# Sliding-window attention and a squared-ReLU MLP on one core: the third batch turned on TensorE, no band matmuls, and an instruction order read from a table

## The chip, the core and the metric

The kernel runs on one core of a Trainium2 chip. The metric is the device time of one launch in microseconds (us). The kernel before takes 298.31 us, the median of three runs (298.27 to 298.75).

## What is computed

Eight batches of eight heads, 576 positions, head size 64. Each position attends to the positions at most 32 away. The heads are then laid side by side (512 columns, 4608 tokens), and an MLP without bias follows, with the square of a ReLU between two matrices.

```python
scores = scale * np.matmul(q, k.transpose(0, 1, 3, 2))      # scale = 1/8
mask = np.abs(pos[:, None] - pos[None, :]) <= 32
attn = softmax(np.where(mask, scores, -1e9))
x = np.matmul(attn, v).transpose(0, 2, 1, 3).reshape(4608, 512)
h = x @ w_in                      # 512 x 2048
r = np.maximum(h, 0.0)
out = (r * r) @ w_out             # 2048 x 512, float32 out
```

## The kernel before

**Groups.** The attention is cut into 24 groups G of 192 tokens, three to a batch. Group G loads its rows of q and k (`load_qk`, L537, issued by GpSimd with a cast to bf16) into one of four `raw` buffers, and a window of 256 rows of v (`load_v`, L563) into one of five `v` buffers. The rows have to be turned so that the head dimension lies on the partitions. For batches 0 and 1, TensorE does this by transposing matmuls (`turn_pe`, L596, eight per turned piece) and ScalarE or VectorE copies the result into the buffer `kq` (L607, L608). From batch 2 on, SyncE issues DMAs that transpose while they move (`turn_dma`, L622, two per group). There are two `kq` buffers, for even and odd batches. A `raw` buffer is free for a later load when its rows have been turned.

**Scores and values.** `scores` makes two blocks of keys per group, A and B (L661, eight matmuls a block). For groups 0 to 2 it first adds the band as a matmul of a bias table with the identity (L653, two 128x512 matmuls a block), and ScalarE's exponential is then the end (L677). For all other groups the exponential (L682) is followed by a multiplication with a 0/1 mask on VectorE (L686). `pv` multiplies with v (L712) and VectorE normalises (L726, L730). A clearing copy (L736) readies the PSUM region between the two blocks.

**Turning the result.** The rows of x go into `xt` turned: by TensorE for groups 0 to 5 (`xturn`, L752 and L758, one copy L766 or L768), by transposing DMAs on SyncE from group 6 on (L771, L774).

**MLP.** `xt` feeds the first layer: plain matmuls (`mm1`, L808) for tokens up to 3584, in pieces of 192, 256 and 512 tokens, and a scheme with seven products instead of eight for the last two blocks of 512 (`mm1s`, L870). ReLU (L787) and square (L782) follow. The second layer is plain for the first 512 tokens (`mm2`, L927), and a seven-product scheme for the others (`strassen`, `product`, L1003, with a copy L1035 that seeds the second bank, and copies and sums L792, L1026). ScalarE issues the stores (L939). While data is still coming in, `fill` puts small matmuls on zeros (L462) into TensorE's gaps.

**What sets the order.** Every operation is recorded with its engine, reads, writes and a key. `plan` (L126 on) then runs a list scheduler with assumed durations, picks for each engine the operation that can start first (ties by key), gives out buffers and PSUM banks, and so fixes one instruction sequence per engine. `emit` writes it with semaphore waits. SyncE, GpSimd and ScalarE work through their queues in that order: an instruction that waits holds all behind it. `OPEN` is the order of the first loads.

Of the kernel before, what the change touches and what calls it, by code (L numbers as in the profile page):

```python
# [1 line left out]

# [3 lines left out]
ALU = mybir.AluOpType  # L6
# [18 lines left out]
    BIAS=110.0,  # L25
    LS=12.75,
    LAG=9.0,
    OG=[0.0, 0.25, 2.5, -0.5, 5.25, 3.5, -7.25, -7.5, -9.0, -18.75, -5.5, 9.75, -6.5, -8.25, 1.5, 0.25, -7.25, -8.75, -7.75, -4.5, 4.75, -1.0, -1.75, -0.75],
    OL=[4.25, 5.25, -0.25, 4.0, 2.75, 0.5, 10.75, 9.5, 7.0, -2.25, -2.25, 3.25, -2.0, 5.25, 7.0, -0.25, 5.75, 3.0, 8.75, -0.25, 7.25, -1.5, 3.5, 0.75],
    OS=[6.5, 2.75, -2.25, -4.5, -2.25, 1.25, 0.75, -0.5, -2.25],  # L30
    O1=[6.5, 7.0, 9.75, -1.25, -4.75, 1.0, 6.25, -0.25, -2.0],
    LEAD=13.0,
    AHEAD=14.5,
    NTURN=2,
    NXT=6,
    NSPLIT=6,
    NPM=3,
# [5 lines left out]
    NUE=3,  # L43
    NRT=4,
    NOE=3,
    WARM=40000,
    TSLACK=1000,
    LSLACK=500,
# [18 lines left out]
class Prog:  # L67
# [58 lines left out]
    def plan(self):  # L126
        cfg, ops = self.cfg, self.ops
        for op in ops:
            op.succ, op.left, op.ready = [], 0, 0
        for op in ops:  # L130
            for d in op.deps | op.order:
                d.succ.append(op)
                op.left += 1
            for u in op.uses:
                u.left = len(u.users)
        t = 0
        for op in sorted((o for o in ops if o.eng == "PE"), key=lambda o: (o.key, o.i)):
            op.late = t
            t += op.dur
        for op in reversed(ops):  # L140
            if op.eng == "PE":
                continue
            op.late = min((s.late - (op.lat if op in s.deps else 0) for s in op.succ), default=t + 5000) - op.dur
            if op.eng in ("ACT", "DVE") and op.dma is None and op.key > -50:
                op.key = op.late / 1000 - cfg["BIAS"]
        engs = ("PE", "ACT", "DVE", "POOL", "SP")
        free = {e: 900 for e in engs}
        free["POOL"] = 1350
        cand = {e: [] for e in engs}
        best = {e: None for e in engs}  # L150
        dirty = {e: True for e in engs}
        slots = {}
        for n, k in self.pools.items():
            slots[n] = [[0, None, False] for _ in range(k)]
        bank = slots["bank"]
        warm = cfg["WARM"]
        bank[7][0] = warm
        self.out = out = []
        rings = {"POOL": [], "SP": [], "ACT": []}
        order = ["POOL", "SP", "ACT"]  # L160
        now = spent = 0.0

        def push(op):
            cand[op.eng].append(op)
            dirty[op.eng] = True
            if op.alt:
                cand[op.alt[0]].append(op)
                dirty[op.alt[0]] = True

        def done(op, end):  # L170
            op.end = end
            for s in op.succ:
                if op.dma is not None or op.eng != s.eng or op.eng != "PE":
                    s.ready = max(s.ready, end)
                else:
                    s.ready = max(s.ready, free[op.eng])
                s.left -= 1
                if not s.left:
                    push(s)
            for u in op.uses:  # L180
                u.left -= 1
                u.free = max(u.free, end)
                if not u.left:
                    for x in u.slot:
                        sl = slots[u.pool][x]
                        sl[0] = u.free
                        sl[1] = u
                        if u.pool == "bank":
                            sl[2] = u.clean
                    for e in engs:  # L190
                        dirty[e] = True

        def find(u, taken):
            ss = slots[u.pool]
            if u.pool != "bank":
                got = None
                for x in range(len(ss)):
                    f = ss[x][0]
                    if f < 1e14 and (got is None or f < got[0]) and (u.pool, x) not in taken:
                        got = (f, (x,))  # L200
                return got
            w = u.where if u.where is not None else range(8)
            got = None
            if u.n == 2:
                for x in range(0, 8, 2):
                    if x in w and ("bank", x) not in taken and ("bank", x + 1) not in taken:
                        f = max(ss[x][0], ss[x + 1][0])
                        r = f + (250 if u.need and not ss[x + 1][2] else 0)
                        if f < 1e14 and (got is None or r < got[2]):
                            got = (f, (x, x + 1), r)  # L210
            else:
                for x in w:
                    f = ss[x][0]
                    if f < 1e14 and ("bank", x) not in taken:
                        r = (f, 0 if ss[x ^ 1][0] > 1e14 else 1, x)
                        if got is None or r < got[2]:
                            got = (f, (x,), r)
            return got and got[:2]

        def grab(op, r):  # L220
            taken, res = (), []
            for u in op.acq:
                g = find(u, taken)
                if g is None:
                    return None
                if g[0] > r:
                    r = g[0]
                res.append(g[1])
                taken = taken + tuple((u.pool, x) for x in g[1])
            return r, res  # L230

        def look(e):
            t, pick = None, None
# [947 lines left out]
```

## Time and profile before

| | before |
|---|---|
| median of three runs | 298.31 us |
| the profiled execution | 298.29 us |
| its span (first to last instruction) | 296.5 us |
| mean granted TensorE clock | 0.994 |
| TensorE matmuls busy | 281.7 us (95%) |
| VectorE, ScalarE, GpSimd busy | 213.5, 186.5, 117.4 us |
| moved by DMA | 40.35 MB |

PE is TensorE's matmuls, PEld its weight loads, DVE VectorE, ACT ScalarE, POOL GpSimd, SP SyncE; a letter q behind an engine is its queue of DMA issues. A row of the timeline has the start and duration in us, the engine, the line, what is written from what, how many instructions, and in brackets the idle time ahead of it and what ended that. Matmuls overlap, so that the step from one start to the next is what one costs, not its duration. Some matmul records are missing from the trace: a count of 3 or 7 where the code has 4 or 8.

### The profile page before, as it was taken

How to read it: one execution, taken by the hardware profiler on the slowest of the kernel's cores; microseconds unless marked ns; L12 is line 12 of the kernel's file. 1: busy time of each engine (PE TensorE's matmuls, PEld its weight loads, DVE VectorE, ACT ScalarE, POOL GpSimd, SP SyncE). 2: the span in 40 equal slices, each digit the busy share in tenths (PEclk: the TensorE clock that was granted, in tenths of full speed). 3: DMA queues.
4: the chain of work that ended last, by engine and by line, in shares of the span. 5: the costliest groups of instructions: out<-in, count | busy, mean ns of one | idle time of the engine just before them, and what ended most of it. 6: DMA issues, size and time to landing. Idle time of an engine off the chain costs nothing.

```text
span 296.5 us, 7164 instructions
## 1 busy us (share of the span) xinstructions
PE 281.7 (95%) x2827; PEld 211.6 (71%) x2850; DVE 213.5 (72%) x444; ACT 186.5 (63%) x298; POOL 117.4 (40%) x153
## 2 busy tenths in 40 slices
PE   6989999999599999999999999999999999999995
PEld 5778667877376467646666656666579888888884
DVE  6457869858765786679677877686889799569811
ACT  3577457978536765786577666656875586288330
POOL 8999489856553454456636453200000000000000
PEclk9999999999889999999999999999999999999999
DMA  9999999999999999999999999999612301211133
GB/s 149 170 199 206 187 154 196 154 169 155 137 177 151 176 139 182 188 153 133 165 156 177 166 175 172 152 157 158 136 35 65 123 3 38 71 38 35 38 107 106
DMA packets 178401, 40.35 MB, mean 136 GB/s; under 512 B 165568, under 2 KB 177856, under 8 KB 178368
## 3 DMA queue, kind: packets, MB, share of 16 engines
q0 software_dynamic: 121920, 18.98, 90.4%
q1 hardware_dynamic: 45600, 11.08, 30.2%
q10 hardware_dynamic: 10848, 9.83, 10.8%
q8 instruction: 22, 0.36, 0.5%
q14 instruction: 11, 0.09, 0.1%
HBM read 38.80 MB, written 9.44 MB: 163 GB/s over the span
## 4 chain that ended last, share of the span: by engine, by line
PE 72%; DMA 12%; POOL 9%; ACT 2%; DVE 2%; issue 2%; ACTq 0%; SPq 0%; POOLq 0%; DVEq 0%
PE ps L1003 33%; PE ps L808 24%; PE ps L870 8%; DMA raw<-in_k_dram 6%; DMA kq<-raw 6%; POOL raw L537 4%; PE ps L661 3%; PE ps L712 3%; POOL v L563 3%; POOL w L575 1%; POOL w L570 1%; DVE gt L782 1%; ACT rt L787 1%; ACT ps L1035 0%; ACT oe L792 0%
## 5 line engine op out<-in xcount | busy, mean ns | idle before, releaser
L808 PE MATMUL ps<-xt,w 128*128 128x512 bf16 (+2 forms) x625 | 104.4, 314 | 1.3 <-DMA w<-in_moe_w_in_dram 0.2
L787 ACT ACTIVATE rt<-ps 128x512 bf16<-128x512 f32 (+1 forms) x127 | 71.9, 572 | 37.3 <-PE ps L808 30.2
L808 PEld LDWEIGHTS ps<-xt,w 128*128 128x128 bf16 x640 | 56.5, 98 | 30.5 <-DMA w<-in_moe_w_in_dram 0.4
L782 DVE TENSOR_TENSOR gt<-rt 128x512 bf16<-128x512 bf16 (+1 forms) x112 | 43.6, 404 | 22.5 <-ACT rt L787 20.0
L563 POOL DMA_DIRECT2D v<-in_v_dram x48 | 41.0, 864 | 38.3 <-PE ps L712 34.7
L1003 PE MATMUL ps<-w,gt 128*128 128x256 bf16 x384 | 49.5, 279 | 1.0 <-ACT ps L1035 0.8
L537 POOL DMA_DIRECT2D raw<-in_k_dram x46 | 36.0, 793 | 29.6 <-DMA kq<-raw 27.0
L682 ACT ACTIVATE e<-ps 128x1024 bf16<-128x1024 f32 x42 | 40.9, 1021 | 10.2 <-PE ps L661 10.2
L1003 PEld LDWEIGHTS ps<-w,gt 128*128 128x128 bf16 x384 | 37.4, 100 | 8.7 <-ACT ps L1035 1.1
L537 POOL DMA_DIRECT2D raw<-in_q_dram x46 | 36.0, 790 | 0.8 <-issue 0.8
L686 DVE TENSOR_TENSOR pt<-e,mask 128x1024 bf16<-128x1024 bf16 x42 | 28.4, 686 | 8.6 <-ACT e L682 8.2
L1003 PE MATMUL ps<-ts,gt 128*128 128x256 bf16 x256 | 31.9, 273 | 0.0
L1003 PE MATMUL ps<-ts,ss 128*128 128x256 bf16 x256 | 31.4, 273 | 0.0
L1003 PEld LDWEIGHTS ps<-ts,gt 128*128 128x128 bf16 x256 | 24.9, 98 | 4.7
L1003 PEld LDWEIGHTS ps<-ts,ss 128*128 128x128 bf16 x256 | 24.4, 98 | 4.0
L792 ACT ACTIVATE ue<-ps 128x512 f32<-128x512 f32 x30 | 17.9, 596 | 9.9 <-PE ps L1003 7.4
L792 ACT ACTIVATE oe<-ps 128x512 f32<-128x512 f32 x19 | 11.3, 597 | 17.1 <-PE ps L1003 16.4
L712 PEld LDWEIGHTS ps<-v,pt 128*128 128x128 bf16 x384 | 17.9, 98 | 5.2 <-issue 0.3
L726 DVE RECIPROCAL rs<-ps 64x8 f32<-64x8 f32 (+1 forms) x48 | 10.0, 209 | 15.0 <-PE ps L712 13.9
L712 PE MATMUL ps<-v,pt 128*128 128x65 bf16 x384 | 20.2, 194 | 0.0
L661 PE MATMUL ps<-kq 64*128 64x128 bf16 x384 | 15.9, 217 | 4.2 <-DMA kq<-raw 4.2
L661 PEld LDWEIGHTS ps<-kq 64*128 64x128 bf16 x384 | 10.9, 94 | 12.1 <-issue 8.6
(71 smaller groups left out, 315.0 us busy)
## 6 DMA issues: line engine op xcount, KB each, us to landing
out_dram<-oe ACTq DMA_DIRECT2D x36, 256.0 KB, 6.1
v<-in_v_dram POOLq DMA_DIRECT2D x32, 128.0 KB, 20.8
raw<-in_q_dram POOLq DMA_DIRECT2D x22, 96.0 KB, 19.2
w<-in_moe_w_in_dram POOLq DMA_DIRECT2D x4, 512.0 KB, 10.6
w<-in_moe_w_out_dram POOLq DMA_DIRECT2D x4, 512.0 KB, 17.0
raw<-in_k_dram POOLq DMA_DIRECT2D x14, 112.0 KB, 19.5
v<-in_v_dram POOLq DMA_DIRECT2D x16, 96.0 KB, 19.5
raw<-in_k_dram POOLq DMA_DIRECT2D x16, 96.0 KB, 20.0
```

The source lines that it names most:

```text
L537: self.p.rec("POOL", lambda e, j=j, dst=dst: e.dma_start(dst, s[:, j]), writes=[self.rtag(t, b, g, j)], dma=(f"{t}{G % self.cfg['NRAW']}{j ...
L563: self.p.rec("POOL", lambda e, j=j, lo=lo, hi=hi, k0=k0: e.dma_start(vt[lo - k0:hi - k0, j, :, 0:64], self.v[b, :, lo:hi, :].rearrange("h ...
L661: mm = e.matmul(sc[:, 512 * par + 128 * j:512 * par + 128 * j + 128], kq[r:r + 64, j, k0:k0 + 128], q, start=not pm and j == 0, stop=True, ...
L682: self.p.rec("ACT", lambda e, ef=ef, v=v: e.activation(ef()[:], self.bank(v, 0, 2), ACTF.Exp, scale=0.125), reads=[v], writes=[ev], key=ke ...
L686: self.p.rec("DVE", lambda e, pf=pf, ef=ef, mb=mb: e.tensor_tensor(pf()[:], ef()[:].rearrange("p (h q) -> p h q", h=8), mb, ALU.mult), rea ...
L712: mm = e.matmul(ps[z:z + n, c:c + 65], ptt[:, 4 * (h % 2) + h // 2, z:z + n], vt[:, w, h, 0:65], start=((w == 0 or (z == 64 and split)) an ...
L782: self.p.rec("DVE", lambda e: e.tensor_tensor(dst, src(), src(), ALU.mult), reads=rd, writes=wr, key=key, dur=dve(c), name=name, alt=alt, ...
L787: self.p.rec("ACT", lambda e: e.activation(dst(), src(), ACTF.Relu), reads=rd, writes=wr, key=key, dur=act(c), name=name, alt=alt, bias=se ...
L792: self.p.rec("ACT", lambda e: e.activation(dst(), src(), ACTF.Copy), reads=rd, writes=wr, key=key, dur=act(c), name=name, alt=alt, bias=se ...
L808: mm = e.matmul(ht[:, n * x:n * x + n], self.W1[:, ft, 128 * d:128 * d + 128], self.XT[:, ft, r:r + n], start=(ft == 0 and x == 0), stop=( ...
L870: mm = e.matmul(bk[:, 256 * x:256 * x + 256], lhs(k, 256 * m + 128 * x), rhs[:, k, :], start=start and x == 0 and k == 0, stop=(k == 1), s ...
L1003: mm = e.matmul(op[:, 256 * y:256 * y + 256], lhs[:, l0[0] + k, a:a + 128], rhs[:, r0 + k, c0:c0 + 256], start=start and y == 0 and k == 0 ...
```

## The change

Six things change.

- `turn_pe` turns groups 6 to 8 (batch 2) as well, and `xturn` turns their rows of x on TensorE (`NTG=9`, `NXT=9`). The transposing DMAs of that batch, six of `kq` and six of `xt`, are gone.
- No group has band matmuls (`NPM=0`): groups 0 to 2 take the exponential and mask path of the others.
- q of batch 1 is loaded in the pieces that k has (224, 192 and 160 rows instead of 192 each).
- The first loads stand in another order.
- Buffers: the three `ue` and three `oe` buffers are one pool of six, the four `rt` and two `hb` buffers another.
- `plan` is gone. `apply` reads the engine, the place in time and the buffer of each recorded operation from a string `ORDER`. The numbers there only sort; the waits come from the data and the buffers as before. The durations that `rec` still carries (82 for a weight load, 28.6 for a transposing DMA) no longer set anything.

```diff
-    NTURN=2,
-    NXT=6,
+    NTG=9,
+    PAIR=(),
+    NXT=9,
-    NPM=3,
+    NPM=0,
-    NUE=3,
-    NRT=4,
-    NOE=3,
+    NRT=6,
+    NOE=6,
...
+    def apply(self, order):
+        order = iter(order.split())
+        last = {}
+        for op in self.ops:
+            s = next(order)
+            op.start = int(s[1:])
+            e = "PADGS".index(s[0])
+            op.eng_ = ("PE", "ACT", "DVE", "POOL", "SP")[e]
+            if op.eng_ != op.eng:
+                op.dur, op.fn = op.alt[1], op.alt[2]
+            op.eng = op.eng_
+        virts = dict.fromkeys(u for op in self.ops for u in op.uses)
+        for u in virts:
+            s = next(order)
+            u.wash = s[-1] == "w"
+            u.slot = tuple(range(int(s.rstrip("w")), int(s.rstrip("w")) + u.n))
+        self.out = sorted(self.ops, key=lambda o: (o.start, o.i))
+        for op in self.out:
             for u in op.acq:
...
                 for x in u.slot:
+                    old = last.get((u.pool, x))
+                    if old is not None:
+                        op.order.update(old.users)
+                    last[u.pool, x] = u
...
     def piece(self, t, b, g):
-        return (192 * g, 192) if t == "q" and b < self.cfg["NTURN"] else KC[g]
+        return (192 * g, 192) if t == "q" and not b else KC[g]
...
-            pe = b < cfg["NTURN"]
+            pe = G < cfg["NTG"]
             turn = 0.6 if pe else 3
...
-        self.p.plan()
+        self.p.apply(ORDER)
...
+OPEN = [("k", 0, "SP", "DVE", 0), ("q", 0), ("k", 1), ("q", 1), ("k", 2), ("q", 2, "ACT", "ACT", 2), ("v", 0), ("v", 1),
+        ("w1", 0), ("w1", 1), ("w1", 2), ("w1", 3), ("w2", 1), ("w2", 0), ("v", 2), ("w2", 2), ("w2", 3)]
+ORDER = """
+D900 G2138 A1350 D2835 D3355 D3775 D4195 D4825 D5245 D5665 D6085 D1100 D2130 D1845 D2350 D1460 D2550 D3055 D5045 D5445
...
```

(Only a line of the table is shown.) How this moves instructions is seen at three places.

**TensorE at the scores of group 8.** In the listings a name's number is its buffer; `kq0` holds the even batches. The kernel before, from a piece of the plain second layer to the first pair of products of the seven-product scheme; the second `ps<-kq0` row is group 8's scores:

```order
L927 MATMUL ps<-w2,gt 128x512 x4
L661 MATMUL ps<-kq0 128x128 x16
L808 MATMUL ps<-xt,w1 128x256 x8
L927 MATMUL ps<-w2,gt 128x512 x8
L712 MATMUL ps<-v2,pt2 128x65 x8
L661 MATMUL ps<-kq0 128x128 x16
L712 MATMUL ps<-v2,pt0 128x65 x8
L1003 MATMUL ps<-w2,gt 128x256 x16
```

And the changed kernel, where L417 is `turn_pe`, L482 the scores, L533 `pv`, L573 and L579 `xturn` and L632 `mm1`:

```order
L573 MATMUL ps<-ident,xa0 128x64 x4
L417 MATMUL ps<-ident,raw0 128x80 x8
L579 MATMUL ps<-ident,xb1 128x128 x4
L533 MATMUL ps<-v1,pt2 128x65 x8
L417 MATMUL ps<-ident,raw0 128x80 x8
L632 MATMUL ps<-xt,w1 128x256 x16
L579 MATMUL ps<-ident,xb0 128x128 x4
L482 MATMUL ps<-kq0 128x128 x16
L632 MATMUL ps<-xt,w1 128x256 x8
L632 MATMUL ps<-xt,w1 128x512 x8
```

The two turns of group 8 (`raw0`) and the turns of x now stand on TensorE, sixteen first-layer matmuls lie between the second turn and the scores, and first-layer matmuls of 512 columns follow where the seven-product scheme began.

**TensorE at the scores of batch 5.** `kq1` now holds batch 5; the kernel before, from group 15's scores (the first `ps<-kq1` row) to group 16's (the last):

```order
L661 MATMUL ps<-kq1 128x128 x16
L1003 MATMUL ps<-w2,gt 128x256 x8
L808 MATMUL ps<-xt,w1 128x512 x8
L712 MATMUL ps<-v0,pt0 128x65 x8
L1003 MATMUL ps<-ts1,ss1 128x256 x8
L808 MATMUL ps<-xt,w1 128x512 x4
L1003 MATMUL ps<-ts1,ss1 128x256 x8
L808 MATMUL ps<-xt,w1 128x512 x4
L712 MATMUL ps<-v0,pt1 128x65 x8
L1003 MATMUL ps<-ts0,ss0 128x256 x8
L808 MATMUL ps<-xt,w1 128x512 x4
L661 MATMUL ps<-kq1 128x128 x16
```

In the changed kernel (L826 is the seven-product scheme) from group 14's scores, the row with `kq0`, on; here the first `kq1` row is group 16's scores and the second is group 15's:

```order
L482 MATMUL ps<-kq0 128x128 x16
L826 MATMUL ps<-ts2,gt 128x256 x8
L826 MATMUL ps<-w2,gt 128x256 x8
L826 MATMUL ps<-ts2,gt 128x256 x8
L482 MATMUL ps<-kq1 128x128 x16
L826 MATMUL ps<-w2,gt 128x256 x8
L826 MATMUL ps<-ts3,gt 128x256 x16
L826 MATMUL ps<-w2,gt 128x256 x16
L533 MATMUL ps<-v4,pt1 128x65 x8
L482 MATMUL ps<-kq1 128x128 x16
```

Group 16's scores, which read the turned rows of groups 15 and 16, have moved ahead of group 15's, to three half products behind group 14's.

**SyncE's queue from its first transposing DMA on.** The kernel before; `kq0` is batch 2 at first, and `kq1` batch 3:

```order
L622 DMA_TRANSPOSE kq0<-raw2 128x8x112 x2
L622 DMA_TRANSPOSE kq0<-raw3 128x8x96 x2
L622 DMA_TRANSPOSE kq0<-raw0 128x8x80
L771 DMA_TRANSPOSE xt<-xa0 128x4x64
L622 DMA_TRANSPOSE kq0<-raw0 128x8x80
L774 DMA_TRANSPOSE xt<-xb0 128x4x128
L622 DMA_TRANSPOSE kq1<-raw1 128x8x112 x2
L771 DMA_TRANSPOSE xt<-xa1 128x4x64
L774 DMA_TRANSPOSE xt<-xb1 128x4x128
L771 DMA_TRANSPOSE xt<-xa2 128x4x64
L774 DMA_TRANSPOSE xt<-xb2 128x4x128
```

The changed kernel (L443 is `turn_dma`, L592 and L595 are `xturn`), where the first row is already batch 3 and `kq0` batch 4:

```order
L443 DMA_TRANSPOSE kq1<-raw1 128x8x112 x2
L443 DMA_TRANSPOSE kq1<-raw2 128x8x96
L443 DMA_TRANSPOSE kq1<-raw3 128x8x80
L443 DMA_TRANSPOSE kq1<-raw2 128x8x96
L443 DMA_TRANSPOSE kq1<-raw3 128x8x80
L592 DMA_TRANSPOSE xt<-xa0 128x4x64
L443 DMA_TRANSPOSE kq0<-raw0 128x8x112 x2
L443 DMA_TRANSPOSE kq0<-raw1 128x8x96
L595 DMA_TRANSPOSE xt<-xb0 128x4x128
```

Batch 3's six transposes stand together with none of `xt` between them, and batch 4's come behind the first half of group 9's x (`xa0`).

More of the change, by code (lines that the diff above doesn't have):

```diff
@@ L570, in load_w1 @@
         self.p.rec("POOL", lambda e: e.dma_start(self.W1[:, :, 512 * d:512 * d + 512], src),
-                   writes=[("w1", d)], dma=(f"w1{d}", 0), key=key, dur=780, move=(32, 79), name=f"w1{d}")
+                   writes=[("w1", d)], dma=(f"w1{d}", 0), key=key, dur=780, move=(32, 82), name=f"w1{d}")
     def load_w2(self, d, key):
@@ L575, in load_w2 @@
         self.p.rec("POOL", lambda e: e.dma_start(self.W2[:, 4 * d:4 * d + 4, :], src),
-                   writes=[("w2", d)], dma=(f"w2{d}", 0), key=key, dur=780, move=(32, 79), name=f"w2{d}")
+                   writes=[("w2", d)], dma=(f"w2{d}", 0), key=key, dur=780, move=(32, 82), name=f"w2{d}")
     def turned(self, t, b, g, x=None):
@@ L801, in mm1, with f @@
         gsteps = [(t0 // 64 + x) % (GRING // 64) for x in range(n // 64)]
[L802 to L816 removed]
+        nb = 2 if pair else 1
+        v = Virt("bank", nb, clean=c >= 512, where=self.cfg.get("MB"))
+        for h in range(nb):
+            dh = ds[h:h + 1] if pair else ds
+            def f(e, h=h, dh=dh):
+                ht = self.bank(v, h)
+                for x, d in enumerate(dh):
+                    for ft in range(4):
+                        mm = e.matmul(ht[:, n * x:n * x + n], self.W1[:, ft, 128 * d:128 * d + 128], self.XT[:, ft, r:r + n],
+                                      start=(ft == 0 and x == 0), stop=(ft == 3), skip_group_check=True)
+                return mm
+            self.p.rec("PE", f, reads=[("xt", s) for s in steps] + [("w1", d // 4) for d in dh[:1]], writes=[(v, h)], uses=[v], key=key + 0.25 * h,
+                       dur=4 * len(dh) * (n / 2.4 + 2.5), name=f"A{t0}.{dh[0]}")
+        rt = Virt("rt", nb)
+        tags = [(v, h) for h in range(nb)]
+        self.relu(lambda: self.rt(rt)[:, 0:c], lambda: self.bank(v, 0, nb)[:, 0:c], tags, [rt], key, f"r{t0}.{d0}", c, uses=[v])
+        self.square(lambda: self.rt(rt)[:, 0:c].rearrange("p (d t) -> p d t", d=len(ds)),
                     gt[:, d0:d0 + len(ds), rg:rg + n], [rt], [("gt", s, d) for s in gsteps for d in ds], key, f"g{t0}.{d0}", c)
@@ L932, in mm2 @@
         oe = Virt("oe")
-        self.copy(lambda: self.OE[oe.slot[0]][:], lambda: self.bank(v), [v], [oe], key, f"o{u}")
-        self.store(u, oe, self.out[128 * u:128 * u + 128, :], lambda: self.OE[oe.slot[0]][:], key, (8, 80))
+        self.copy(lambda: self.oe(oe), lambda: self.bank(v), [v], [oe], key, f"o{u}")
+        self.store(u, oe, self.out[128 * u:128 * u + 128, :], lambda: self.oe(oe), key, (8, 42))
     def store(self, u, oe, dst, src, key, move):
@@ L1118, in record @@
             m = 512 // n
+            if t0 in cfg["PAIR"]:
+                for x in range(8):
+                    d = 2 * (x // 2) + 8 * (x % 2)
+                    key = t0 / 64 + x + cfg["O1"][t0 // 512]
+                    at(t0 / 64 + x, self.mm1, t0, n, [d, d + 1], key, True)
+                t0 += n
+                continue
             for x, d in enumerate(range(0, 16, m)):
```

393 lines of the change are left out of this document (138 added, 255 removed), and 8 rows, old and new, of the table ORDER.

## The prediction

> **What bounds the kernel now.** I read the page first, then TensorE's waits, its timeline around the longest of them, and the windows there.
>
> ```profile
> PE 281.7 (95%) x2827; PEld 211.6 (71%) x2850; DVE 213.5 (72%) x444; ACT 186.5 (63%) x298; POOL 117.4 (40%) x153
> DMA  9999999999999999999999999999612301211133
> ```
>
> TensorE is busy for 95% of the span, so it is the engine that sets the end, and the DMA engines are full until about slice 29, some 210 us. Time can go only where TensorE stands still, runs slowly or has work taken from it. TensorE's waits name two sources of size:
>
> ```profile
> PE ps L661 <- DMA kq<-raw: 4.2, 2, 3.6
> PE ps L1003 <- ACT ps L1035: 0.8, 2, 0.4
> ```
>
> The scores (L661) wait twice for transposing DMAs. TensorE's timeline has the places:
>
> ```profile
> 63.90 0.62 PE L661 MATMUL ps<-kq 64*128 64x128 bf16 x16 [0.59 <-DMA kq<-raw]
> ...
> 75.21 0.42 PE L712 MATMUL ps<-v,pt 128*128 128x65 bf16 x8
> 79.20 0.62 PE L661 MATMUL ps<-kq 64*128 64x128 bf16 x16 [3.58 <-DMA kq<-raw]
> ...
> 80.06 3.53 PE L1003 MATMUL ps<-w,gt 128*128 128x256 bf16 x16
> ...
> 84.26 1.92 PE L1003 MATMUL ps<-w,gt 128*128 128x256 bf16 x16 [0.42 <-ACT ps L1035]
> ```
>
> Both are scores of the third batch, groups 6 and 8, and the rows of that batch are what the change turns on TensorE. Sixteen products take 3.53 us right behind the long wait and 1.92 us a little later: the wait has a tail. The windows say why:
>
> ```profile
> 19.00:75.00 56.00, 54.27 (x654) 42.55 (x658) 43.07 (x95) 40.00 (x67) 43.19 (x56) 1.00 1.88 176
> 75.00:80.00 5.00, 1.42 (x33) 1.11 (x32) 3.37 (x7) 1.47 (x4) 1.86 (x4) 1.00 1.82 126
> 80.00:83.50 3.50, 3.50 (x25) 2.55 (x22) 2.66 (x5) 1.80 (x2) 2.25 (x3) 0.52 1.50 203
> 75.00:210.00 135.00, 129.49 (x1163) 85.86 (x1177) 98.70 (x197) 87.36 (x136) 56.20 (x72) 0.99 1.76 163
> ```
>
> The columns are the window, its length, busy PE, PEld, DVE, ACT and POOL, the granted clock, the DMA share and GB/s. From 80.0 to 83.5 the clock is 0.52, and 1.00 before.
>
> **The change part by part.** Sums are made against the profiled execution, 298.29 us: a span of 296.5 and 1.8 around it. The median of the three runs is 298.31, so nothing has to be corrected.
>
> *The third batch's waits.* The chain of waits has the second transpose of group 8:
>
> ```profile
> 70.49 8.58 DMA kq<-raw
> ```
>
> It was issued at 70.5, so that the rows had landed by then. Turn and copy take about a microsecond on TensorE's path, and the scores could follow from 71.5; TensorE came to them at 75.6. So nothing is late in place of this wait. Gone: 3.6 for the wait, 3.53 - 1.92 = 1.6 for the half clock behind it, 0.6 for group 6. Sum -5.8. If the load itself were late, at most the 3.6 and 1.6 would stay.
>
> *TensorE's new work.* What one turned piece costs, and what turning a group's x costs, is read from one start to the next:
>
> ```profile
> 37.74 0.29 PE L752 MATMUL ps<-ident,xa 64*128 64x64 bf16 x4
> 37.95 0.43 PE L712 MATMUL ps<-v,pt 128*128 128x65 bf16 x8
> ...
> 41.55 0.39 PE L758 MATMUL ps<-ident,xb 128*128 128x128 bf16 x4
> 41.77 1.03 PE L927 MATMUL ps<-w,gt 128*128 128x512 bf16 x4
> ...
> 43.95 0.51 PE L596 MATMUL ps<-ident,raw 96*128 96x96 bf16 x8
> 44.30 0.82 PE L808 MATMUL ps<-xt,w 128*128 128x192 bf16 x8
> ...
> 47.89 0.45 PE L596 MATMUL ps<-ident,raw 80*128 80x80 bf16 x8 [0.52 <-DMA raw<-in_k_dram]
> ```
>
> Eight turns of mean width (96) take 0.35; six pieces are 2.1. A group's x takes 0.21 + 0.22 = 0.43; three are 1.3. All of it lies on the engine that sets the end: +3.4. The wait of 0.52 at 47.89 is the turn of k of group 5, which the new order puts behind more other work: -0.6 with the 0.1 behind it; if it stays, 0.
>
> *Their copies, and the masks.* Six more copies to `kq`, three to `xt`, and six mask multiplications that the band matmuls had spared:
>
> ```profile
> L686 DVE TENSOR_TENSOR pt<-e,mask 128x1024 bf16<-128x1024 bf16 x42 | 28.4, 686 | 8.6 <-ACT e L682 8.2
> ...
> L608 DVE COPY kq<-ps 128x768 bf16<-128x768 bf16 x5 | 2.8, 556 | 3.8 <-PE ps L596 3.6
> ...
> L607 ACT ACTIVATE kq<-ps 128x768 bf16<-128x768 bf16 x3 | 2.4, 810 | 1.9 <-PE ps L596 1.9
> ```
>
> Nine copies at 0.56 (VectorE) to 0.81 (ScalarE) are 5.0 to 7.3 us, six masks at 0.69 are 4.1. They hide: between 19 and 75 us VectorE is idle for 12.9 of 56 us and ScalarE for 16.0. I take 0; if half the copies' time came through as waits of TensorE it would be +3.1.
>
> *The opening.*
>
> ```profile
> 18.18 0.45 PE L596 MATMUL ps<-ident,raw 80*128 80x80 bf16 x8 [1.11 <-DMA raw<-in_k_dram]
> ...
> 22.19 0.59 PE L653 MATMUL ps<-bias,ident 128*128 128x512 bf16 x2
> ...
> 23.91 4.13 PE L808 MATMUL ps<-xt,w 128*128 128x192 bf16 x48
> ```
>
> Before, four first-layer pieces run from 19 to 22 us, then group 2's scores with two band pairs, and the fifth piece starts at 23.91. In the new order twelve loads of rows stand ahead of the three weight chunks that the first five pieces need, against ten and two in another mix before; the bytes ahead of the third chunk are the same. Its issue and its time to landing before:
>
> ```profile
> 12.49 0.80 POOL L575 DMA_DIRECT2D w<-in_moe_w_out_dram  x1
> ```
>
> ```profile
> w<-in_moe_w_out_dram POOLq DMA_DIRECT2D x1, 512.0 KB, 10.7
> ```
>
> So it lands at 23.2 in both orders, now it is one of `w_in`, and the fifth piece can start then, with the bands out of the way: -0.7. The other end is +0.7, one mask multiplication (0.69, above) more in the chain from the first scores to `xt`. I take -0.7, since the first pieces ran from 19 us on before, 4 us ahead of that landing, so that the chain has room.
>
> *The order.* At both early seeds of the seven-product scheme (L1035) the table puts first-layer matmuls between the first and the second product: -0.8 from the row of the waits; 0 if another wait takes their place.
>
> *The scores of group 16, the new wait.* They now stand right behind group 14's, ahead of group 15's. TensorE reached group 14's scores, and SyncE issued the transposes of group 16's rows, so:
>
> ```profile
> 139.08 0.62 PE L661 MATMUL ps<-kq 64*128 64x128 bf16 x16
> ```
>
> ```profile
> 139.86 2.28 SPq L622 DMA_TRANSPOSE kq<-raw  x1
> 144.01 1.21 SPq L771 DMA_TRANSPOSE xt<-xa  x1
> 145.36 1.32 SPq L622 DMA_TRANSPOSE kq<-raw  x1
> ```
>
> ```profile
> kq<-raw SPq DMA_TRANSPOSE x1, 9.8
> ```
>
> The second one landed at 145.36 + 9.8 = 155.2. The sum so far is -5.8 + 3.4 - 0.6 - 0.7 - 0.8 = -4.5. So TensorE is now due at 139.1 + 0.55 - 4.5 = 135.1 (the three half products that it does first were done ahead of 139.08 before). How far do the transposes move up? From the DMA queues in a stretch without transposes (38 to 50 us) and one full of them (86 to 200 us); the numbers are packets, MB and share:
>
> ```profile
> q0 software_dynamic: 13666, 1.72, 225.1%
> q10 hardware_dynamic: 144, 0.26, 6.6%
> ```
>
> ```profile
> q0 software_dynamic: 62585, 7.86, 116.7%
> q1 hardware_dynamic: 29184, 7.08, 52.2%
> q10 hardware_dynamic: 3536, 3.41, 9.8%
> ```
>
> Loads and a store: 12 us for 1.98 MB, 6.1 us per MB. In the second stretch the loads' 7.86 MB are 48 us of 114, and 66 us are left for 10.49 MB, 6.3 per MB. The twelve DMAs that are gone moved 1.77 MB (576 rows of 1024 and of 512 bf16), 11.1 us of the full DMA engines. Two and a half pairs of `xt` transposes that stood ahead of this one on SyncE now stand behind it, 0.2 MB or 1.2 us each: 3.0. That gives 155.2 - 14.1 = 141.1, a wait of 6.0. But the second transpose was also issued 5.5 us behind the first only because a transpose of x, waiting for VectorE, stood between them; in the new order it is the x of two groups earlier. Then it is 135.6, a wait of 0.5. I take 0.5, since the queue's wait is in the rows and its cause is moved, and keep 0 to 6.0.
>
> [...]
>
> **The sum.** 298.29 - 4.5 + 0.5 = 294.3.
>
> **The rivals.** A measurement of this kernel can tell 0.2%, 0.6 us, from no change.
>
> *The forecast:* the third batch's waits go, TensorE pays 3.4, and what waits come are about those that went elsewhere. 291.5 to 297.2 (the top has a wait of 3.4 at group 16, just short of the half clock); chance 0.74. The low end is 294.3 less the 0.5, less the rest of TensorE's idle time from 75 to 210 us (135.00 - 129.49 = 5.5, of which 3.6 and 0.8 are already in the sum: 1.1), less 1.2 if the opening also saves the wait of 1.11 at 18.18.
>
> *The copies come through:* TensorE waits for half of the nine copies, +3.1, 297.4. For it: between 19 and 75 us VectorE is busy for 77% already. Against: the turns stand well ahead of the scores that read them. Chance 0.15; in two of three such cases still faster by over 0.2%.
>
> *The wait moves to group 16, slower:* the scores of batch 5 are asked for earlier than SyncE's queue delivers. At 6.0 us TensorE also loses the clock, as it did behind 3.58: 293.8 + 6.0 + 1.6 = 301.4. It decides from a wait of 2.9 with the half clock, 4.5 without. For it: the new order brings scores forward by more than the change frees. Against: loads can be issued earlier, since `raw` buffers no longer wait for a DMA in batch 2. Chance 0.09.
>
> [...] The bytes and times above speak against it: chance 0.02.
>
> Together: faster 0.74 + 0.10 = 0.84, same 0.05, slower 0.02 + 0.09 = 0.11. The range for 8 in 10 runs from 291.5 to 298.8: above it lie the two slow cases (0.11), below it perhaps 0.05. The top is the case of the copies, 297.4, with the opening at its bad end, 1.4 more.
>
> **What would show it.** In the profile of the changed kernel: no wait of the scores for DMA between 55 and 80 us, and a clock of 1.00 from 75 to 90; 48 more turning matmuls of `kq` and 24 more of `xt` on TensorE; the fifth first-layer piece near 23.2; the scores of group 16 near 135 with a wait under 1 us; q1 with 1.77 MB less. Wrong it would be with a wait of several microseconds for `kq<-raw` after 100 us, with TensorE waiting for `kq` or `xt` copies, or with a second stretch at half clock.

## The result, and the profile after

| | before | after |
|---|---|---|
| median (runs) | 298.41 us (4) | 293.50 us (4) |
| range | 298.27 to 298.75 | 293.22 to 293.69 |
| ratio, 95% interval | | 0.9833 [0.9816, 0.985] |
| the profiled execution, its span | 298.29, 296.5 | 293.44, 291.6 |

The forecast was 294.3 us, between 291.5 and 298.8. The changed kernel is faster by 4.9 us. A ratio leaves out executions that took over 1.5% longer than the fastest of the same kernel; further down these are one of the four of turn_alone_refit and four of the ten of all_but_table_refit, the profiled one among them, so that there a median of all lies above what the ratio gives.

First the page of the changed kernel: busy times, the granted clock, the DMA engines, and the queue of the transposing DMAs.

```profile
PE 284.4 (98%) x2956; PEld 216.3 (74%) x2956; DVE 215.8 (74%) x440; ACT 197.3 (68%) x313; POOL 117.5 (40%) x153
PEclk9999999999999999999999999999999999999999
DMA  9999999999999999999999999996021320301123
q1 hardware_dynamic: 38304, 9.31, 26.1%
```

TensorE does more (284.4 against 281.7 us) in a shorter span, never at a lower clock, and q1 moves 1.77 MB less than 11.08, as reckoned. TensorE's waits (all but that of the scores, L482, lie in the opening, ahead of 19 us), then the windows that answer to those of before:

```profile
PE ps L283 <- DVE zz L277: 1.2, 1, 1.2
PE ps L417 <- DVE raw L373: 1.2, 1, 1.2
PE ps L482 <- DMA kq<-raw: 0.7, 1, 0.7
PE ps L632 <- DMA w<-in_moe_w_in_dram: 0.2, 1, 0.2
PE ps L573 <- DVE xa L551: 0.2, 1, 0.2
```

```profile
19.00:75.00 56.00, 55.92 (x725) 45.04 (x725) 45.36 (x98) 42.27 (x71) 45.04 (x57) 1.00 1.97 177
75.00:80.00 5.00, 5.00 (x54) 3.26 (x52) 4.55 (x9) 4.46 (x7) 5.00 (x8) 1.00 1.92 173
80.00:83.50 3.50, 3.50 (x37) 1.77 (x36) 3.37 (x8) 3.15 (x6) 2.58 (x4) 1.00 1.88 155
75.00:210.00 135.00, 134.25 (x1238) 90.38 (x1236) 98.76 (x191) 98.16 (x152) 54.63 (x70) 1.00 1.60 154
```

From 75 to 80 us TensorE was busy for 1.42 us before and is for all 5.00 now; from 80 to 83.5 the clock is 1.00 instead of 0.52. In the long window its idle time falls from 5.51 to 0.75 us, from 19 to 75 us from 1.73 to 0.08. The 0.75 left are the one wait that the prediction had added, at group 16's scores. TensorE's timeline has it and group 8's turns and scores; SyncE's timeline has the two transposing DMAs of group 16, the second of which it waits for, and the DMA view its time to landing:

```profile
72.55 0.46 PE L417 MATMUL ps<-ident,raw 80*128 80x80 bf16 x8
72.89 0.40 PE L579 MATMUL ps<-ident,xb 128*128 128x128 bf16 x4
73.13 0.42 PE L533 MATMUL ps<-v,pt 128*128 128x65 bf16 x8
73.38 0.45 PE L417 MATMUL ps<-ident,raw 80*128 80x80 bf16 x8
73.67 1.91 PE L632 MATMUL ps<-xt,w 128*128 128x256 bf16 x16
75.42 0.39 PE L579 MATMUL ps<-ident,xb 128*128 128x128 bf16 x4
75.74 0.62 PE L482 MATMUL ps<-kq 64*128 64x128 bf16 x16
...
79.16 3.61 PE L632 MATMUL ps<-xt,w 128*128 128x512 bf16 x16
...
135.10 0.62 PE L482 MATMUL ps<-kq 64*128 64x128 bf16 x16 [0.75 <-DMA kq<-raw]
```

```profile
123.33 1.22 SPq L443 DMA_TRANSPOSE kq<-raw  x1
...
125.95 1.31 SPq L443 DMA_TRANSPOSE kq<-raw  x1
```

```profile
kq<-raw SPq DMA_TRANSPOSE x1, 8.8
```

A turn of group 8 costs 0.34 and 0.29 us from start to start, one of x 0.24, and its scores follow at 75.74 without a wait. The second transposing DMA of group 16 was issued at 125.95 instead of 145.36 and landed 8.8 us later, at 134.75.

One difference was in no view that the prediction quotes. How long TensorE spends on the first layer (its line alone), first in the kernel before and then in the changed one:

```profile
73.00:92.00 19.00, 0.65 (x6) 0.91 1.87 149
```

```profile
73.00:92.00 19.00, 12.08 (x64) 1.00 1.96 160
```

Before, that stretch has hardly any first-layer matmuls. The block of tokens 1024 to 1535 needs the x of groups 5 to 7; the last DMA that turned x of group 7 was issued at 83.15 and landed 6.6 us later, at 89.8:

```profile
83.15 1.19 SPq L774 DMA_TRANSPOSE xt<-xb  x1
```

```profile
xt<-xb SPq DMA_TRANSPOSE x1, 6.6
```

Now TensorE has done the last turn of group 7's x by 73.1 and of group 6's by 75.7 (the rows of L579 above), and the block is under way at 79.16. So the 19 us around the wait for group 8's transposes now hold 12 us of first-layer work.

### The profile page after: what moved, and what is told of

It reads as the page before. It is cut to its first block, busy times and chain, and to the rows that moved or that the text cites. A ratio compares the mean times of both kernels' runs of the same rounds, so it can differ in the third digit from the quotient of the medians.

```text
span 291.6 us, 7363 instructions
## 1 busy us (share of the span) xinstructions
PE 284.4 (98%) x2956; PEld 216.3 (74%) x2956; DVE 215.8 (74%) x440; ACT 197.3 (68%) x313; POOL 117.5 (40%) x153
## 3 DMA queue, kind: packets, MB, share of 16 engines
q0 software_dynamic: 121920, 18.98, 89.8%
## 4 chain that ended last, share of the span: by engine, by line
PE 87%; DMA 7%; POOL 4%; SPq 0%; issue 0%; ACT 0%; POOLq 0%
PE ps L826 32%; PE ps L632 31%; PE ps L695 8%; PE ps L750 5%; PE ps L482 4%; PE ps L533 4%; DMA w<-in_moe_w_in_dram 4%; DMA kq<-raw 3%; POOL raw L358 2%; PE ps L417 2%; POOL v L384 1%; PE ps L579 1%; PE ps L573 1%; POOL w L391 1%; SPq L592 0%
## 5 line engine op out<-in xcount | busy, mean ns | idle before, releaser
L632 PE MATMUL ps<-xt,w 128*128 128x512 bf16 (+2 forms) x640 | 105.4, 315 | 0.3 <-DMA w<-in_moe_w_in_dram 0.2
L608 ACT ACTIVATE rt<-ps 128x512 bf16<-128x512 f32 (+1 forms) x122 | 69.0, 570 | 28.2 <-PE ps L632 23.6
L632 PEld LDWEIGHTS ps<-xt,w 128*128 128x128 bf16 x640 | 56.7, 98 | 33.3 <-issue 0.3
L503 ACT ACTIVATE e<-ps 128x1024 bf16<-128x1024 f32 x48 | 47.5, 1022 | 8.8 <-PE ps L482 4.8
L603 DVE TENSOR_TENSOR gt<-rt 128x512 bf16<-128x512 bf16 (+1 forms) x96 | 38.0, 402 | 16.0 <-ACT rt L608 14.8
L826 PE MATMUL ps<-w,gt 128*128 128x256 bf16 x384 | 45.9, 273 | 0.0
L613 ACT ACTIVATE oe<-ps 128x512 f32<-128x512 f32 x47 | 27.5, 597 | 22.0 <-PE ps L826 19.8
L826 PEld LDWEIGHTS ps<-w,gt 128*128 128x128 bf16 x384 | 36.9, 98 | 5.1
L507 DVE TENSOR_TENSOR pt<-e,mask 128x1024 bf16<-128x1024 bf16 x48 | 33.0, 687 | 8.2 <-ACT e L503 7.7
L826 PE MATMUL ps<-ts,ss 128*128 128x256 bf16 x256 | 31.9, 273 | 0.0
L826 PE MATMUL ps<-ts,gt 128*128 128x256 bf16 x256 | 31.3, 273 | 0.0
L826 PEld LDWEIGHTS ps<-ts,ss 128*128 128x128 bf16 x256 | 24.3, 98 | 4.7
L826 PEld LDWEIGHTS ps<-ts,gt 128*128 128x128 bf16 x256 | 24.4, 98 | 3.9
L602 ACT ACTIVATE gt<-rt 128x512 bf16<-128x512 bf16 (+1 forms) x40 | 24.4, 614 | 2.9 <-DVE rt L607 2.0
L533 PEld LDWEIGHTS ps<-v,pt 128*128 128x128 bf16 x384 | 17.8, 98 | 5.4 <-issue 0.3
L533 PE MATMUL ps<-v,pt 128*128 128x65 bf16 x384 | 19.9, 194 | 0.1
L547 DVE RECIPROCAL rs<-ps 64x8 f32<-64x8 f32 (+1 forms) x48 | 10.0, 207 | 11.0 <-PE ps L533 10.1
L551 DVE TENSOR_TENSOR xa<-ps,rs 64x512 bf16<-64x512 f32 x24 | 16.7, 695 | 0.8
L551 DVE TENSOR_TENSOR xb<-ps,rs 128x512 bf16<-128x512 f32 x24 | 16.5, 687 | 0.4
```

The lines of the kernel that those rows point to most:

```text
L503: self.p.rec("ACT", lambda e, ef=ef, v=v: e.activation(ef()[:], self.bank(v, 0, 2), ACTF.Exp, scale=0.125), reads=[v], writes=[ev], key=ke ...
L507: self.p.rec("DVE", lambda e, pf=pf, ef=ef, mb=mb: e.tensor_tensor(pf()[:], ef()[:].rearrange("p (h q) -> p h q", h=8), mb, ALU.mult), rea ...
L533: mm = e.matmul(ps[z:z + n, c:c + 65], ptt[:, 4 * (h % 2) + h // 2, z:z + n], vt[:, w, h, 0:65], start=((w == 0 or (z == 64 and split)) an ...
L551: p.rec("DVE", lambda e, rs=rs, r0=r0, m=m, x=x: e.tensor_tensor(x[r0:128, :].rearrange("p (x y c) -> p x y c", x=2, y=4), view(r0, m).rea ...
L602: alt = ("ACT", act(c), lambda e: e.activation(dst, src(), ACTF.Square)) if self.cfg["ALT"] else None
L603: self.p.rec("DVE", lambda e: e.tensor_tensor(dst, src(), src(), ALU.mult), reads=rd, writes=wr, key=key, dur=dve(c), name=name, alt=alt, ...
```

## The experiments

The question: is the gain the removed waits of the third batch less TensorE's turns, each part worth what it is worth alone (my theory), or does the table make it (rival one), or the band matmuls with the opening (rival two)? All kernels were timed beside the kernel before, which had medians of 298.42 to 299.04 us; the results:

| run | us, median (range) | ratio to before, 95% interval |
|---|---|---|
| turn_alone | 304.68 (304.28 to 305.22) | 1.0208 [1.0182, 1.0235] |
| all_but_table | 303.63 (302.14 to 304.63) | 1.0174 [1.0131, 1.0217] |
| keys_by_dma | 304.11 (303.71 to 305.15) | 1.0199 [1.0172, 1.0227] |
| x_by_dma | 304.44 (303.57 to 305.52) | 1.0207 [1.0175, 1.0239] |
| bands_back | 294.69 (294.64 to 296.25) | 0.9879 [0.9846, 0.9912] |
| sixteen_later | 293.54 (293.32 to 293.88) | 0.9834 [0.9802, 0.9867] |
| third_chunk_later | 294.20 (293.61 to 294.33) | 0.9851 [0.9821, 0.9881] |
| two_edits | 294.69 (293.26 to 296.12) | 0.987 [0.9832, 0.9907] |
| turn_alone_refit | 303.04 (300.17 to 305.45) | 1.0125 [1.004, 1.0211] |
| all_but_table_refit | 298.20 (295.52 to 301.74) | 0.9961 [0.9929, 0.9993] |
| before_refit | 298.95 (297.41 to 300.92) | 1.0005 [0.9974, 1.0037] |
| scores_later | 300.96 (299.25 to 301.98) | 1.0065 [1.0036, 1.0094] |

In the last four the executions of one kernel differ by more. The new buffer pools, the pieces of q and the order of the loads were not varied alone.

### The turn without the table

turn_alone is the kernel before with this edit:

```diff
-            pe = b < cfg["NTURN"]
+            pe = G < 9
...
-    NXT=6,
+    NXT=9,
```

> The kernel before with one edit: the keys, queries and x of the third batch (groups 6 to 8) are turned on TensorE; planner, load order and band matmuls as before. My theory (the gain is the third batch's waits on transposing DMAs, less TensorE's extra turns): the 3.58 us wait at 79.20, the half clock after it (1.6) and the 0.59 at 63.9 go, TensorE gets 3.1 to 3.4 us of turns, the opening's fifth first-layer piece stays at 23.9 and the seeds stay: 295.9 us, 294.9 to 296.9. Rival one (the searched table makes the gain, turning alone is immaterial): the planner finds new waits for what it lost, 297.8 us or more. Rival two (the band matmuls and the opening make the gain): 298.0 to 298.8, since both stay.

all_but_table is the changed kernel with the planner, its settings and the load order of before (the main line of the edit):

```diff
-        self.p.apply(ORDER)
+        self.p.plan()
```

> The changed kernel with everything but the table: third batch turned on TensorE, no band matmuls, new pools, but the order comes from the planner before with its settings and its load order. My theory: waits of the third batch gone (-5.8), turns added (+3.1 to 3.4), seeds gone (-0.8), opening unchanged or 0.7 earlier: 295.0 us, 294.2 to 296.2. Rival one (the table makes the gain): 297.5 us or more. Rival two (bands and opening): about as the changed kernel, 293.3 to 294.0, with the fifth first-layer piece at 23.4 or earlier.

Both are some 5 to 6 us slower than before. My theory fell here, by 9 us, and so did rival two, by 6 to 10; rival one's bounds held. The part of my account that speaks of the third batch held all the same: turn_alone's TensorE is busy for 15.00 of the 15 us from 75 to 90 (before 11.00) at full clock. The time is lost later:

```profile
75.00:90.00 15.00, 15.00 (x139) 8.74 (x138) 14.07 (x30) 12.48 (x21) 12.51 (x16) 1.00 1.93 160
...
140.00:152.00 12.00, 7.81 (x84) 5.84 (x81) 7.31 (x15) 4.85 (x7) 8.71 (x11) 0.72 1.71 168
```

```profile
143.39 1.04 PE L661 MATMUL ps<-kq 64*128 64x128 bf16 x16 [2.34 <-issue]
145.61 1.89 PE L1003 MATMUL ps<-w,gt 128*128 128x256 bf16 x8 [1.18 <-ACT e L682]
```

In those 12 us TensorE stands still for 4.19 and runs at a clock of 0.72, where before it was busy for 11.89 at 1.00. Its timeline there shows scores, products with v and products of the second layer, each close behind the last, and not one first-layer matmul from 136.0 to 163.14: the planner, with the offsets of the kernel before, had spent or put off that work. The stages add up: from 75 to 90 us turn_alone gains 4.0 us of idle time and 1.65 of half clock; it pays about 3.4 for the turns (the forecast's price), and from 140 to 210 us it loses 5.3 of idle time and 3.4 of half clock. That makes 6.4; the medians differ by 6.3, the spans of the two profiled executions by 6.9. all_but_table loses 3.66 us between 135 and 150 in the same way.

### The table without the turn

keys_by_dma is the changed kernel with the keys and queries of groups 6 to 8 back in transposing DMAs, x_by_dma with the x of those groups back:

```diff
-            pe = G < cfg["NTG"]
+            pe = G < 6
```

> The changed kernel with its table, but the keys and queries of the third batch are turned by six transposing DMAs again, issued ahead of the next batch's. TensorE loses six turns of 0.34 us (-2.1). My theory: the scores of groups 6 to 8, which the table places at 62 to 76 us, wait for landings 8 to 10 us after the loads, one wait of over 3 us with a half-clock stretch behind it (+1.6), and the queue behind is later by six transfers, so that group 16's scores at 135 wait longer: 298.5 us, 296.5 to 301.5. Rival one (the table makes the gain, the kind of turning does not matter): 291.4 to 293.7, no wait above 1 us at those scores.

```diff
-    NXT=9,
+    NXT=6,
```

> The changed kernel with its table, but the x of groups 6 to 8 is turned by six transposing DMAs. TensorE loses six turns of 0.22 to 0.43 us (-1.05). My theory: the first-layer pieces of the third batch's first token block, which the table places right behind, wait for x, once by 2 to 4 us, with up to 1 us of half clock behind it: 295.5 us, 293.8 to 297.5. Rival one (turning is immaterial): 292.0 to 292.7, no wait for x above 0.5 us.

In the table, the entries of the turns and their copies give way to entries for the DMAs; the times of all others stay.

The direction was my theory's and the size was far above it: 304.11 against 298.5 us, and 304.44 against 295.5, both above the stated ranges. One row of TensorE's timeline in each has the wait:

```profile
71.19 1.04 PE L482 MATMUL ps<-kq 64*128 64x128 bf16 x16 [9.14 <-DMA kq<-raw]
```

```profile
87.96 3.33 PE L632 MATMUL ps<-xt,w 128*128 128x512 bf16 x8 [11.47 <-DMA xt<-xb]
```

Behind both the clock is lower (0.67 from 72 to 80 us in keys_by_dma, 0.64 from 88 to 92 in x_by_dma), as the scores' 1.04 us (0.62 at full clock) and eight first-layer matmuls in 3.33 us (1.89) show. The chain of waits says why the waits are so long:

```profile
62.72 8.33 DMA kq<-raw
```

```profile
78.62 9.10 DMA xt<-xb
```

Each time the latency of one transposing DMA, 8 to 9 us, lies bare, because the table has nothing else in that place. I had priced the waits at over 3 us and at 2 to 4 us. In the kernel before, the wait had been 3.58 us, and the other 5.0 of that DMA's 8.58 were covered by other work. These runs are harsh on the DMA: the table was made for a batch that it does not turn, and in x_by_dma the late DMA, issued at 78.62, also stood behind two other transposes on SyncE, issued from 74.83 on. They show that this table needs the turn, not what the best table without it would do. Rival one (at most 293.7) fell in both.

### An order fitted to each

With the turn and the table each losing alone, the next question was whether the planner does as well when its offsets fit. In three kernels they were chosen anew, by a search over the planner's own plans, of which one was run for each kernel; in turn_alone_refit, for instance:

```diff
-    LS=12.75,
-    LAG=9.0,
-    OG=[0.0, 0.25, 2.5, -0.5, 5.25, 3.5, -7.25, -7.5, -9.0, -18.75, -5.5, 9.75, -6.5, -8.25, 1.5, 0.25, -7.25, -8.75, -7.75, -4.5, 4.75, -1.0, -1.75, -0.75],
...
+    LS=9.25,
+    LAG=8.0,
...
```

> As the run with the turn alone (planner, pools, band matmuls of the kernel before; third batch turned on TensorE), but the planner's offsets of groups, loads and blocks are chosen anew for the turned batch; they had been those fitted to the batch turned by DMAs, and with them the work on TensorE between 130 and 150 us had thinned out (first-layer matmuls 3.8 us of 20). Theory now (the turn pays as reckoned, once the order is fitted to it): no stretch of waits at 140, 296.0 us, 295.0 to 297.0. Rival (the fine order of the table makes the gain, the turn only makes room for it): fitting brings back what the kernel before had and no more, 297.5 to 299.5 us.

> As the run with all but the table (third batch turned, no band matmuls, new pools, planner), with the planner's offsets chosen anew for it. Theory now: the turn's gain of some 2.4 us and the bands' 1.2 us both show: 294.8 us, 293.8 to 295.8. Rival (the table's fine order makes the gain): 296.5 us or more.

> The control: the kernel before, nothing turned anew, no other part of the change, with its planner's offsets chosen anew in the same way. Theory now (fitting by itself brings nothing that the kernel before did not have): 298.4 us, 297.4 to 299.5. Rival (choosing the order anew makes the gain, with or without the turn): 296.5 us or less.

The control is at 1.0005 of before, as expected: choosing anew brought nothing by itself. With the turn alone it is no cure either (303.04, range 300.17 to 305.45): beyond even the rival's bounds. With the rest of the change it comes to 0.9961 of before: rival one's side, though far better than 303.63. Both had single waits in new places; these are the two large ones of turn_alone_refit and the one of all_but_table_refit:

```profile
155.26 0.42 PE L712 MATMUL ps<-v,pt 128*128 128x65 bf16 x8 [2.75 <-DMA v<-in_v_dram]
168.54 0.62 PE L661 MATMUL ps<-kq 64*128 64x128 bf16 x16 [2.19 <-ACT oe L792]
```

```profile
198.79 0.58 PE L743 MATMUL ps<-v,pt 128*128 128x65 bf16 x8 [3.12 <-DMA v<-in_v_dram]
...
195.00:202.00 7.00, 3.88 (x33) 1.76 (x31) 2.34 (x6) 2.26 (x4) 0.00 (x0) 0.77 0.60 78
```

(The last row is from the windows.) GpSimd's timeline has the last two loads of v issued at 171.80 and 173.78, 27.0 and 25.0 us ahead of the end of that wait. Without that wait and the half clock behind it, an estimate of 4.7 us (3.12 of idle time, and 7 us at 0.77), this execution of 300.30 would be near 295.6. The others took 295.52 to 301.74, and none of them has a trace: whether they have this wait, and so what sets the ratio of 0.9961, is not shown.

### An order without the turn

scores_later is the kernel before with one stretch of its order changed by hand. TensorE's order from the product of group 7 on, before (-) and in this kernel (+):

```diff
-L712 MATMUL ps<-v,pt 128x65 x8
-L661 MATMUL ps<-kq 128x128 x16
-L712 MATMUL ps<-v,pt 128x65 x8
-L1003 MATMUL ps<-w,gt 128x256 x16
...
+L712 MATMUL ps<-v,pt 128x65 x16
+L1003 MATMUL ps<-w,gt 128x256 x32
+L661 MATMUL ps<-kq 128x128 x16
+L1003 MATMUL ps<-ts,ss 128x256 x16
```

> The kernel before, nothing turned anew and no other part of the change, with one stretch of its order changed by hand: the scores of group 8 stand behind the product of group 7 and 32 second-layer matmuls, the scores of group 9 behind 40 more, and what follows from both moves with them. Rival (an order that does not ask too early makes the gain, the turn is not needed): the wait of 3.58 and the half clock behind it (1.6) go, nothing takes their place: 293.1 us, 292.5 to 294.2. Theory now (the order and the turn are needed together: with the third batch in the transposing DMAs' queue, TensorE that comes 5 us earlier finds the later transposes no earlier): the waits reappear at the scores of groups 9 to 16, in all 2 to 4 us: 296.3 us, 295.2 to 297.8.

Both were wrong. The DMA wait went, and none came back at groups 9 to 16 (0.5 us for `kq<-raw` in the whole execution, at group 6), but the kernel is slower by 0.65%. TensorE's timeline:

```profile
78.25 0.43 PE L712 MATMUL ps<-v,pt 128*128 128x65 bf16 x8 [2.15 <-ACT ps L736]
79.07 3.13 PE L1003 MATMUL ps<-w,gt 128*128 128x256 bf16 x16 [0.39 <-DVE gt L971]
82.88 1.97 PE L1003 MATMUL ps<-w,gt 128*128 128x256 bf16 x16 [0.67 <-ACT ps L1035]
84.78 0.62 PE L661 MATMUL ps<-kq 64*128 64x128 bf16 x16
...
89.76 0.43 PE L712 MATMUL ps<-v,pt 128*128 128x65 bf16 x8 [1.19 <-ACT ps L736]
...
94.77 2.54 PE L808 MATMUL ps<-xt,w 128*128 128x512 bf16 x11 [1.41 <-ACT e L682]
```

The wait of 3.58 is paid in other coin: 2.15 for the clearing copy between the blocks of group 7, then 0.39 and 0.67 for sums and a seed, the half clock again (16 products in 3.13 us), 1.19 and 1.41 later. Nothing else is there to do: the first layer has 1.05 us of work between 73 and 93, as little as in the kernel before (0.65 between 73 and 92). So that wait was the longest of several latencies in a stretch without other work, and in this order taking it away alone frees nothing.

### The opening

bands_back puts the bias table and the band matmuls back:

```diff
-    NPM=0,
+    NPM=3,
```

> The changed kernel with its table, but the mask of groups 0 to 2 is added on TensorE by band matmuls again, as before, and the six multiplications by the mask on VectorE and GpSimd go. My theory: the opening waits for the third chunk of the first layer's weights (landing at 23.36) whether TensorE does band matmuls or idle ones until then, so nothing changes: 293.5 us, 293.2 to 293.9. Rival two (the band matmuls make the gain): their 48 matmuls come back on the path, 294.5 to 296.1 us.

Rival two's time was right: 1.2 us slower than the changed kernel. The bands are twelve matmuls, not 48: six pairs of some 0.54 us from start to start, 3.2 us in all. With 1.2 of the 4.9 us they are a part of the gain in this table, but do not make it, and all_but_table is slow without them. The timeline of TensorE has the fifth first-layer piece at 25.44, 2.0 us behind the changed kernel's 23.40, and none of TensorE's waits in this run is for a chunk of weights:

```profile
18.70 0.59 PE L474 MATMUL ps<-bias,ident 128*128 128x512 bf16 x2
19.23 0.40 PE L482 MATMUL ps<-kq 64*128 64x128 bf16 x8
...
20.42 0.83 PE L632 MATMUL ps<-xt,w 128*128 128x192 bf16 x8
...
25.44 2.80 PE L632 MATMUL ps<-xt,w 128*128 128x192 bf16 x32
```

In the table's order the bands stand ahead of the first pieces, and the chain to the fifth has no room for them. Some 0.8 of the 2.0 us come back later: the wait at group 16 is gone in this run. Nor is all of it the bands' own: the chain of waits from 18.05 to 25.44 holds 2.1 us of idle matmuls, which the table's times place and which TensorE works through in turn, such as

```profile
22.30 0.67 PE ps L283 x12
```

An order made for the bands might lose less; that was not tried.

third_chunk_later exchanges two loads of the table (the names ahead of the entries are added here):

```diff
-w10 G12908  v020 G13688
+w10 G13700  v020 G12908
```

> The changed kernel, with two loads of the opening exchanged: the third chunk of the first layer's weights behind 0.08 MB of the values of group 2, which puts its landing about 0.8 us later. My theory (that landing sets when the opening's first-layer work goes on, and idle matmuls fill the time before): the fifth piece starts at 24.15 and all behind it is 0.8 us later: 294.3 us, 294.0 to 294.6. Rival (the opening has slack that later stages absorb): 293.3 to 293.7 us.

294.20 against 293.50, within my theory's range. The fifth piece, first in the changed kernel and then here, started 0.5 us later, behind a wait of 0.91 for the chunk:

```profile
23.40 2.81 PE L632 MATMUL ps<-xt,w 128*128 128x192 bf16 x32
```

```profile
23.92 2.81 PE L632 MATMUL ps<-xt,w 128*128 128x192 bf16 x32 [0.91 <-DMA w<-in_moe_w_in_dram]
```

So that landing is on the path in the changed kernel. With the bands back it is not; the chain on TensorE is. The delay need not come through whole: in the profiled execution, at 293.61 the shortest of the six, group 16's scores wait 0.41 us instead of 0.75 and start only 0.17 later than in the changed kernel.

### The wait at group 16

sixteen_later moves the scores by one product in the table (the name is added here):

```diff
-S16B P134634
+S16B P135300
```

> The changed kernel, one place of the table changed: the scores of group 16 stand one second-layer product (0.87 us) later on TensorE. My theory (what is left of the wait at 135 for group 16's transposing DMA is on the path): the wait of 0.75 us goes and nothing takes its place: 292.8 us, 292.6 to 293.1. Rival: the exponentials of group 16 come later as well and the wait reappears at the next scores or products, 293.4 to 293.8 us.

The rival was right: no change. The wait is gone at group 16's scores (the first row) and stands five microseconds on, at the copy that seeds a second-layer product:

```profile
135.07 0.62 PE L482 MATMUL ps<-kq 64*128 64x128 bf16 x16
...
140.82 1.92 PE L826 MATMUL ps<-w,gt 128*128 128x256 bf16 x16 [0.68 <-ACT ps L858]
```

two_edits has the same move and the x of group 8 by transposing DMAs (`NXT=8`).

> The changed kernel with the scores of group 16 one product later, as in the other run, and the x of group 8 turned by transposing DMAs: its users come at 112 us, over 20 us behind its making. My theory: the wait of 0.75 goes, TensorE loses two turns (0.22 and 0.43 us), and the queue behind the two transposing DMAs still lands in time: 292.2 us, 291.9 to 292.8. Rival (every transposing DMA that is put back into SP's queue makes the ones behind it late): the scores of groups 12 to 16 wait, 293.5 to 296 us.

My theory (292.2) fell. The median of 294.69 lies within the rival's bounds, but its mechanism did not show at the scores: the profiled execution waits 1.48 us for a load of v that took 28.5 us:

```profile
177.67 0.41 PE L533 MATMUL ps<-v,pt 128*128 128x65 bf16 x8 [1.48 <-DMA v<-in_v_dram]
```

The six executions spread over 2.9 us (293.26 to 296.12), against 0.6 in sixteen_later, which lacks only the two transposing DMAs. That the late load makes this spread is not shown. No version beat the changed kernel.

## Why the prediction was right, and what in it was not

**What held, as a description of the changed kernel.** The third batch's waits and the half clock went (-5.8), and nothing was late in their place. The six turns (0.29 to 0.39 us from start to start) and three of x (0.22 and 0.24 to 0.32) took 2.1 + 1.5 = 3.6, against 3.4. The wait at group 5's turn and both seeds went (-0.6, -0.8). The copies and masks cost TensorE nothing to be seen: its idle time from 19 to 75 us is 0.08 us. TensorE was ready for group 16's scores at 134.35 and began them at 135.10, a wait of 0.75; the forecast had 135.1, 135.6 and 0.5. The landing moved up by 155.2 - 134.75 = 20.4 us, against 19.6. That this is so near is in part luck: the sum was 14.1 for the bytes and the order, and 5.5 for the gap between the two transposes of the group. The first one moved up by 16.5 (139.86 to 123.33), the gap closed by 2.9 only (from 5.50 to 2.62, with a transpose of x still in it), and the time to landing fell by 1.0.

**What was mis-sized.** The profiled executions differ by 4.85 us, and the forecast was 4.0. The opening brought 0.5 at the fifth piece instead of 0.7, group 16's wait cost 0.25 more and the turns 0.2 more. The small waits between 19 and 75 us gave 0.45 more (idle time 1.73 to 0.08, of which 1.2 was forecast). And TensorE's small idle times from 75 to 210 us, 1.1 in all, went too; I had put them into the low end of the range alone. With these the sum is 4.9. The top of the range took a wait of 3.4 us to be just short of the half clock; no run shows a limit at that length: the clock was 0.50 behind a wait of 2.34 in turn_alone, and 1.00 behind one of 2.85 in before_refit.

**What failed is the claim behind the sum, that each term belongs to its part.** The step on the order credited the table with 0.8 us, the two seeds; the step on the third batch said that nothing would be late in place of the wait. Near the wait this is so in turn_alone as well (75 to 90 us); but of the orders that were run, only in the table's does the time saved there reach the end. With the planner's order the same turns gave a kernel 6.3 us slower (turn_alone), 5.2 with every other part of the change (all_but_table), and only 0.4% under before when the planner's offsets were fitted to it (0.9961). Measured so, the table is worth 10.1 us given the turn (303.63 - 293.50), or 3.8 against the best planned order tried here (0.9961 - 0.9833 of 298.4); and the turn is worth over 10 given this table (keys_by_dma, x_by_dma). In the orders tried here each without the other is a loss or close to nothing, and the gain of 4.9 is neither's alone. What the best table without the turn would bring is open.

**Why the wait could be had back.** The prediction reads the 3.58 at 79.20 as a DMA that comes late. scores_later shows that it stood in a stretch where every latency was bare. What the turn does there, by the trace, is more than to remove a landing: x of groups 6 and 7 is turned by 75.7 instead of 89.8, which lets the first layer's next block fill the stretch (12.08 us instead of 0.65). x_by_dma shows one half of this: with the keys turned on TensorE and x by DMA, the same table stands still until 87.96 ahead of that block. That the filling is what makes the wait recoverable is argued from these traces; a kernel with x turned on TensorE and only the keys by DMA, in an order made for it, was not run. Why the planner's plans leave a bare stretch elsewhere, at 140 us, is shown only as far as their rows go.

**The rivals.** Copies that come through: no sign. The wait that moves to group 16: it did, at 0.75 us and not at 6.0. The slow case with the chance of 0.02, that the removed transposes free little of the queue: refuted by the landing at 134.75, 20.4 us earlier than before.

## What to carry to other kernels

On an engine that is busy for 95%, a wait names what comes last and not what is missing; before pricing its removal, count the work that is ready in that stretch (the line's busy time by windows), since without such work the next latencies take its place, as in scores_later (2.15, 0.39, 0.67, 1.19 and 1.41 us where there had been 3.58). An edit and an order that was fitted to it are one change: reckon them together, and do not carry the edit alone into an order that was fitted without it. In keys_by_dma and x_by_dma a transposing DMA among full DMA engines cost its whole latency, 8.33 and 9.10 us, where no other work covered it.

## What the runs showed of the hardware

In these runs the half clock does not come at one length of wait. The prediction took 3.4 us for safe. In scores_later TensorE's clock is halved behind a wait of 2.15 and one of 0.39 (first row below, a window at 0.50), and in turn_alone behind one of 2.34 (0.50 from 144 to 150 us; the row at 143.39 above: sixteen scores in 1.04 us). In before_refit it stays at 1.00 behind 2.85 (the row of the wait in the timeline, and the window):

```profile
80.00:81.00 1.00, 1.00 (x7) 0.69 (x6) 0.41 (x1) 0.00 (x0) 0.83 (x2) 0.50 1.87 154
```

```profile
82.50 0.62 PE L661 MATMUL ps<-kq 64*128 64x128 bf16 x16 [2.85 <-DMA kq<-raw]
...
82.00:86.00 4.00, 3.09 (x49) 2.70 (x50) 2.82 (x6) 2.52 (x3) 2.63 (x4) 1.00 1.67 193
```

In these rows a longer wait kept the clock and shorter ones lost it; what decides is not shown. In turn_alone 2.34 us were enough, and the sixteen scores behind that wait took 1.04 us instead of 0.62: there the wait cost more than its own length.
